# Four lengths in a kernel's own ordering model set to other values: top-k attention and a rational feed-forward layer on one core

## The chip, the core and the metric

The kernel runs on one core of a Trainium2 chip. The metric is device time in microseconds (us), the median of several executions. One execution was also recorded by the profiler; its rows are what the text reads.

## The reference

The inputs are q, k, v of shape (8 batches, 8 heads, 576 rows, 64), the weights of a layer (512 to 2048 to 512) in float64, and a few coefficients. Cut to what matters:

```python
scores = scale * np.matmul(q, k.transpose(0, 1, 3, 2))          # 576 x 576 per head
kth = np.partition(scores, -32, axis=-1)[..., -32:-31]
scores = np.where(scores >= kth, scores, -1e9)                   # keep the 32 largest of a row
attn = np.exp(scores - scores.max(-1, keepdims=True))
attn = attn / (attn.sum(-1, keepdims=True) + 1e-09)
x = (attn @ v).transpose(0, 2, 1, 3).reshape(4608, 512)
h = x @ w_in                                                     # 4608 x 2048
P = a[0] + a[1]*h + a[2]*h**2 + a[3]*h**3
Q = 1.0 + abs(b[0])*abs(h) + abs(b[1])*h**2
out = (P / (Q + 1e-6)) @ w_out
```

## The kernel before, in words

**Attention.** A tile is 128 query rows of one head (in a name `s_3_0_2_0`: batch 3, row block 0, head pair 2, head 0 of it); two tiles make a unit, and the last 64 rows of both heads make one mixed tile (row block 4). There are 288 tiles. TensorE makes the scores (L575, L572), ScalarE copies them out (`sb`, L582), and VectorE halves the row of 576 to two rows of 288, larger and smaller (`hi`, `lo`, L590 and L586), and takes the eight largest four times, striking them out between (L600, L606); L615 gives the 32nd. ScalarE makes the exponentials (`e`, L640), VectorE masks and sums them (`pr`, L643). TensorE turns `pr` (`trp`, L718 and L720; ScalarE copies out, `p`, L730) and multiplies it by the values (`av`, L744). There is one scores buffer, two `pr` buffers (one for each unit) and two PSUM banks of the tag `mm`, which `trp`, `av` and `ph` share. So the exponentials of a unit wait until all turns of the unit two before it are done.

**Feed-forward.** 256 rows of the attention's output are a chunk (`m2_2`: batch 2, row blocks 2 and 3; `t0`, `t4`: chunks of mixed rows). A chunk is done in eight groups of 256 hidden columns. A group is 24 matmuls into `ph` (L885; three split products for each of 4 x 2 pieces), three or four reads of `ph` by ScalarE, some five elementwise steps on GpSimd, VectorE and ScalarE, and a product with w_out: twelve matmuls for a group of split weights (L1038), four for one in full precision (L1031). From chunk 14 on (`y.late`) the elementwise chain has another form (L268 `hh`, L956 `va`, L959, L963 `pa` on VectorE; on GpSimd L967 and L968 in place of L963), and each step may be taken by more than one engine.

**Weights.** w_in and w_out are converted from float64 words at the start, in blocks of 128 x 512, by ScalarE (L387, L405), VectorE (L392, L399) and GpSimd (L409, L425).

**The order.** No engine's order is written out. `build` makes some twenty thousand steps; `Plan.run` (L83) then walks through them in a time of its own: a step has a length for each engine that may do it, a key (lower goes first), steps that it waits for, and buffers that it takes and gives. An engine that is free in that time takes the ready step of the lowest key whose buffers are free. What the walk decides is emitted: the order on each engine's queue and, where more than one engine may do a step, which one does it. The chip then runs each queue in that order, with its own durations. The lengths stand at L237 to L259, and some of them at the step itself.

The lengths that the change touches are: `pe_r` (L243), for scores (L652), hidden products (`add_group`) and split output products; `dma` (L246), for all transfers on the SP queue; the VectorE steps of the weight conversion in `weight_block` (L379 to L381, which no block of this kernel takes, and L414, L415); and `n_av` (L805), the value products of a unit pair.

```python
    pe_r = lambda n: max(0.107, n / 2400 + 0.003)
    dma = lambda n, words: max(0.52 * n, words * 4 / 180e3)
            m = add("PE", len(cs) * n_av, multiply(cs), [m] if m else pair.ev + [pair.vload], key + KEY['AV'],
```

## Time and profile before

| | |
|---|---|
| median of 3 runs | 1662.68 us (1662.24 to 1662.74) |
| the profiled execution | 1662.6 us, its span 1660.8 us |
| busy in the span: VectorE (DVE) | 1514.2 us, 91% |
| TensorE matmul (PE) | 1455.1 us, 88% |
| TensorE weight load (PEld) | 1138.5 us, 69% |
| ScalarE (ACT) | 1287.4 us, 78% |
| GpSimd (POOL) | 1286.2 us, 77% |
| mean granted TensorE clock | 0.954 |

Busy times are over the whole span, and stages differ: weights are converted in the first 300 us, then attention and feed-forward run side by side, and after the last attention tile (1554.5 us) only feed-forward is left. The span begins at the first recorded instruction; 1.8 us of the execution's time lie outside it.

### The profile page before, as it was taken

What the parts mean: (1) busy time and instruction counts of PE and PEld (TensorE: products, weight loads), DVE (VectorE), ACT (ScalarE), POOL (GpSimd) and SP (SyncE); (2) the same over time, 40 slices, a digit from 0 to 9 for tenths busy, and PEclk for the clock granted to TensorE, in tenths of its full rate; (3) what the DMA queues carried; (4) which work ended last, traced back from release to release, by engine and by line L of the source; (5) the groups of instructions that cost most, each with busy time, mean ns of one, the idle gap of its engine ahead of it and who ended that gap; (6) DMA issues with size and microseconds to landing.
All of it is one profiled execution on the core that took longest, in us unless ns stands there. A gap on an engine that the chain in (4) does not pass through costs nothing.

```text
span 1660.8 us, 31905 instructions
## 1 busy us (share of the span) xinstructions
PE 1455.1 (88%) x9513; PEld 1138.5 (69%) x9513; DVE 1514.2 (91%) x5044; ACT 1287.4 (78%) x2579; POOL 1286.2 (77%) x1649
## 2 busy tenths in 40 slices
PE   2436878899999899999999999998999999898996
PEld 1324656676777678777777777777777778676784
DVE  6989998999999999798899999999999999899753
ACT  4555857887888798787888888888788888777653
POOL 5675877787878698878877897988878988878642
PEclk9657888999999999999999999999999999999998
DMA  6454545334443454325443445344533554231122
GB/s 198 145 165 138 150 128 162 103 92 127 130 118 93 117 145 146 98 72 137 121 122 86 115 139 155 90 112 123 149 94 94 137 144 112 84 92 53 45 61 69
DMA packets 133238, 193.57 MB, mean 117 GB/s; under 512 B 21440, under 2 KB 71616, under 8 KB 133056
## 3 DMA queue, kind: packets, MB, share of 16 engines
q1 hardware_dynamic: 132992, 191.43, 40.6%
q8 instruction: 78, 1.28, 0.3%
q14 instruction: 104, 0.85, 0.2%
q0 software_dynamic: 64, 0.00, 0.0%
HBM read 125.83 MB, written 13.11 MB: 84 GB/s over the span
## 4 chain that ended last, share of the span: by engine, by line
PE 50%; DVE 27%; ACT 9%; POOL 6%; issue 4%; DMA 2%; SPq 1%; ACTq 0%; POOLq 0%; DVEq 0%
PE ph_m L885 14%; DVE m L600 9%; PE po_m L1038 8%; DVE hi L606 7%; PE av L744 7%; PE po_m L1031 6%; PE s L575 6%; PE trp L718 4%; DVE pr L643 4%; DVE lo L586 2%; PE ph_t L885 2%; DVE hi L590 2%; ACT p L730 2%; DVE w_w L399 1%; ACT e L640 1%
## 5 line engine op out<-in xcount | busy, mean ns | idle before, releaser
L600 DVE MAX8 m<-hi 128x8 f32<-128x288 f32 x1152 | 498.9, 451 | 2.4
L606 DVE MATCH_REPLACE8 hi<-m,hi 128x288 f32<-128x288 f32 x864 | 382.6, 445 | 0.1
L885 PE MATMUL ph_m<-xh_m,win_h 128*128 128x256 f32 x1024 | 309.9, 303 | 18.3 <-ACT p L730 12.9
L718 PE MATMUL trp<-ident,pr 128*128 128x128 f32 x1312 | 226.2, 285 | 80.9 <-DVE pr L643 50.2
L885 PE MATMUL ph_m<-xl_m,win_h 128*128 128x256 f32 x1024 | 288.2, 281 | 0.0
L885 PE MATMUL ph_m<-xh_m,win_l 128*128 128x256 f32 x1024 | 288.1, 281 | 0.0
L718 PEld LDWEIGHTS trp<-ident,pr 128*128 128x128 f32 x1312 | 162.9, 145 | 149.6 <-ACT p L730 45.1
L730 ACT COPY p<-trp 128x512 f32<-128x512 f32 (+1 forms) x448 | 227.2, 514 | 47.0 <-PE trp L718 35.7
L643 DVE SCALAR_TENSOR_TENSOR pr<-sb,m,e 128x576 f32<-128x576 f32 x288 | 231.0, 802 | 31.7 <-ACT e L640 29.4
L582 ACT COPY sb<-s 128x576 f32<-128x576 f32 x288 | 185.5, 644 | 95.5 <-PE s L575 81.1
L640 ACT ACTIVATE e<-sb,st 128x576 f32<-128x576 f32 x288 | 216.9, 753 | 40.1 <-DVE pr L643 36.5
L885 PEld LDWEIGHTS ph_m<-xh_m,win_h 128*128 128x128 f32 x1024 | 194.8, 190 | 41.9 <-ACT p L730 24.6
L885 PEld LDWEIGHTS ph_m<-xl_m,win_h 128*128 128x128 f32 x1024 | 195.2, 191 | 4.6 <-issue 3.3
L885 PEld LDWEIGHTS ph_m<-xh_m,win_l 128*128 128x128 f32 x1024 | 194.6, 190 | 0.0
L744 PE MATMUL av<-p,vm 128*64 128x256 f32 (+1 forms) x1920 | 189.1, 346 | 3.5 <-ACT p L730 2.3
L1031 PE MATMUL po_m<-wout,pa_m 128*128 128x512 f32 x384 | 187.8, 595 | 0.0
L907 POOL TENSOR_TENSOR pa_m<-pa_m,hh_m 128x512 f32<-128x512 f32 x104 | 133.9, 1288 | 50.3 <-ACT pa_m L904 49.2
L744 PEld LDWEIGHTS av<-p,vm 128*64 128x64 f32 x1920 | 112.5, 143 | 78.6 <-issue 16.5
L934 POOL TENSOR_TENSOR pa_m<-pa_m,va_m 128x512 f32<-128x512 f32 x104 | 134.1, 1289 | 29.6 <-ACT va_m L931 28.4
L575 PE MATMUL s<-ka,q 128*128 128x288 f32 x512 | 103.7, 327 | 50.0 <-DMA q<-qx 13.5
L590 DVE TENSOR_TENSOR hi<-s,sb 128x288 f32<-128x288 f32 x288 | 129.0, 448 | 17.6 <-ACT sb L582 16.8
L1038 PE MATMUL po_m<-wout,g_m 128*128 128x512 f32 x320 | 138.1, 431 | 1.6 <-ACT ob_m L1056 0.7
(143 smaller groups left out, 3678.2 us busy)
## 6 DMA issues: line engine op xcount, KB each, us to landing
wl_m<-wout_l SPq DMA_DIRECT2D x160, 256.0 KB, 2.7
vm<-in_v_dram SPq DMA_DIRECT2D x96, 320.0 KB, 3.0
q<-qx SPq DMA_DIRECT2D x128, 128.0 KB, 2.5
q<-qx SPq DMA_DIRECT2D x256, 64.0 KB, 2.1
km<-in_qk_dram SPq DMA_DIRECT2D x32, 352.0 KB, 3.3
kl<-in_qk_dram SPq DMA_DIRECT2D x32, 288.0 KB, 3.4
qx<-in_qk_dram SPq DMA_DIRECT2D x64, 128.0 KB, 2.8
w_w<-in_moe_w_in_dram SPq DMA_DIRECT2D x32, 256.0 KB, 3.9
```

The lines of the kernel that those rows point to most:

```text
L575: nc.tensor.matmul(s[:, hf, 0:HF], u.pair.q.q[:, i, t.h, o : o + P], kv.k[t.h][:, cols], start=(i == 0), stop=(i == 1),)
L582: nc.scalar.copy(t.sb, t.s[:, :, 0:HF])
L600: nc.vector.max(t.m[:, o : o + 8], getattr(t, src))
L606: nc.vector.match_replace(x, t.m[:, o : o + 8], x, NEG)
L640: nc.scalar.activation(t.e, t.sb, AF.Exp, scale=SCALE, bias=t.st)
L643: nc.vector.scalar_tensor_tensor(out=t.pr, in0=t.sb, scalar=t.kth, in1=t.e, op0=ALU.is_ge, op1=ALU.mult, accum_out=u.ss[:, t.h : t.h + 1],)
L718: nc.tensor.transpose(u.ps[i][:, c * P : (c + 1) * P], u.pr[:, x], ident)
L730: nc.scalar.copy(pair.pT[i][:, at].rearrange("p c n -> p (c n)"), u.ps[i][:, 0 : n * P])
L744: nc.tensor.matmul(pair.av[d, 0 : u.nq * len(pair.units)], lhs, x[:, 0, d] if u.mixed else x[:, 0] if lone else x, start=(c == 0), stop=(c ...
L885: nc.tensor.matmul(y.ph[:, f * NT : (f + 1) * NT], w[:, c, fs], z[:, c, :], start=(c == 0 and i == 0), stop=(c == HP - 1 and i == 2),)
L1031: nc.tensor.matmul(o.po[i], y.pa[:, at], wout[ff], start=(ff == 0), stop=(ff == NF - 1),)
L1038: nc.tensor.matmul(o.po[i], z, w, start=(ff == 0 and n == 0), stop=(ff == NF - 1 and n == 2),)
```

## The change

Lengths in the planner are set to other values; no instruction is added or removed, and no data is laid out otherwise.

```diff
-    pe_r = lambda n: max(0.107, n / 2400 + 0.003)
+    pe_r = lambda n: max(0.109, n / 2230 + 0.003)
-    dma = lambda n, words: max(0.52 * n, words * 4 / 180e3)
+    dma = lambda n, words: max(0.52 * n, words * 4 / 260e3)
...
-                    s1 = add("DVE", dve(128), upper, [ld], key + 1)
-                    s2 = add("DVE", dve(256), lower, [s1], key + 1)
-                    last.append(add("DVE", dve(256), ends, [s2], key + 2, give=hold if plain else []))
+                    s1 = add("DVE", 0.38, upper, [ld], key + 1)
+                    s2 = add("DVE", 0.5, lower, [s1], key + 1)
+                    last.append(add("DVE", 0.5, ends, [s2], key + 2, give=hold if plain else []))
...
-                s2 = add("DVE", dve(128), high, [s1], key + 1)
-                s3 = add("DVE", dve(256), low, [s2], key + 1)
+                s2 = add("DVE", 0.38, high, [s1], key + 1)
+                s3 = add("DVE", 0.5, low, [s2], key + 1)
...
-        n_av = 1.3 * pe_t if u.mixed else 2.5 * pe_t if lone else 4.42 * pe_t
+        n_av = 1.4 * pe_t if u.mixed else 2.7 * pe_t if lone else 4.6 * pe_t
```

What it does is move instructions, from the first rows on. Four counts change between engines: VectorE gets six more of the additions and products L956, four more L268 `hh` and two more L963, GpSimd six fewer L956; ScalarE passes 32 of the small scalings L272 on to GpSimd's L274. Three places:

**TensorE, the first feed-forward groups beside the mixed tiles of batch 0.** The rows just ahead of the last turn of the mixed tile `0_4_3`, up to that turn. Before:

```order
L885 MATMUL ph_m0_0_2_1640<-xh_m0_0_1352,win_l_79 128x256
L718 MATMUL trp0_0_4_3_1697<-ident_65,pr_0_4_3_1520 128x128 x4
L885 MATMUL ph_m0_0_2_1640<-xh_m0_0_1352,win_h_78 128x256
L885 MATMUL ph_m0_0_2_1640<-xl_m0_0_1353,win_h_78 128x256
L885 MATMUL ph_m0_0_2_1640<-xh_m0_0_1352,win_l_79 128x256
L575 MATMUL s_0_3_0_1_1712<-kb_0_0_132,q_0_0_2_1224 128x288 x4
L718 MATMUL trp2_0_4_3_1724<-ident_65,pr_0_4_3_1520 128x128
L720 MATMUL trp2_0_4_3_1724<-ident_65,rw_0_4_3_1634 128x128
```

Now:

```order
L885 MATMUL ph_m0_0_3_1839<-xh_m0_0_1351,win_l_79 128x256
L718 MATMUL trp0_0_4_3_1887<-ident_65,pr_0_4_3_1677 128x128 x4
L885 MATMUL ph_m0_0_3_1839<-xh_m0_0_1351,win_h_78 128x256
L885 MATMUL ph_m0_0_3_1839<-xl_m0_0_1352,win_h_78 128x256
L885 MATMUL ph_m0_0_3_1839<-xh_m0_0_1351,win_l_79 128x256
L885 MATMUL ph_m0_0_3_1839<-xh_m0_0_1351,win_h_78 128x256
L885 MATMUL ph_m0_0_3_1839<-xl_m0_0_1352,win_h_78 128x256
L885 MATMUL ph_m0_0_3_1839<-xh_m0_0_1351,win_l_79 128x256
L718 MATMUL trp2_0_4_3_1906<-ident_65,pr_0_4_3_1677 128x128
L720 MATMUL trp2_0_4_3_1906<-ident_65,rw_0_4_3_1848 128x128
```

The turn stood behind group 2 of the first chunk and stands behind group 3. Between the scores `s_0_3_0_0` and this turn there were 24 matmuls of `ph` and 10 rows of `av`; there are 48, with 12 of L1038 and 20 rows of `av`.

**TensorE, chunk m2_2, around the scores of the tile `3_1_2_0`.** Before:

```order
L1038 MATMUL po_m2_2_1_8751<-wl_m2_2_3_0_8884,g_m2_2_3_8886 128x512
L575 MATMUL s_3_1_2_0_8963<-ka_3_2_7495,q_3_2_0_8534 128x288 x4
L885 MATMUL ph_m2_2_7_8988<-xh_m2_2_8114,win_h_78 128x256
L885 MATMUL ph_m2_2_7_8988<-xl_m2_2_8115,win_h_78 128x256
L885 MATMUL ph_m2_2_7_8988<-xh_m2_2_8114,win_l_79 128x256
```

Now:

```order
L885 MATMUL ph_m2_2_6_8912<-xl_m2_2_8134,win_h_78 128x256
L885 MATMUL ph_m2_2_6_8912<-xh_m2_2_8133,win_l_79 128x256
L575 MATMUL s_3_1_2_0_8919<-ka_3_2_7533,q_3_2_0_8485 128x288 x4
L885 MATMUL ph_m2_2_6_8912<-xh_m2_2_8133,win_h_78 128x256
L885 MATMUL ph_m2_2_6_8912<-xl_m2_2_8134,win_h_78 128x256
```

At this tile the chunk stood at its last group, 7, and stands at group 6. Between the scores `s_3_0_2_0` and the last turn of unit `3_0_1` there were 57 matmuls of `ph` and 5 of L1031; there are 72 and 8 (L1038: 36 in both).

**VectorE, chunk m6_2, the rows that end with the masking of the tile `7_0_2_0`.** Before:

```order
L615 MAX m_7_1_2_19815<-m_7_1_2_19815 128x8
L963 SCALAR_TENSOR_TENSOR pa_m6_2_5_19851<-pa_m6_2_5_19851,co_70,va_m6_2_5_19848 128x512
L268 TENSOR_SCALAR hh_m6_2_6_19909<-va_m6_2_6_19900,co_70 128x512
L959 TENSOR_TENSOR pa_m6_2_6_19907<-pa_m6_2_6_19907,h_m6_2_6_19886 128x512
L963 SCALAR_TENSOR_TENSOR pa_m6_2_6_19907<-pa_m6_2_6_19907,co_70,h_m6_2_6_19886 128x512
L963 SCALAR_TENSOR_TENSOR pa_m6_2_6_19907<-pa_m6_2_6_19907,co_70,va_m6_2_6_19900 128x512
L959 TENSOR_TENSOR pa_m6_2_7_19944<-pa_m6_2_7_19944,h_m6_2_7_19932 128x512
L963 SCALAR_TENSOR_TENSOR pa_m6_2_7_19944<-pa_m6_2_7_19944,co_70,h_m6_2_7_19932 128x512
L963 SCALAR_TENSOR_TENSOR pa_m6_2_7_19944<-pa_m6_2_7_19944,co_70,va_m6_2_7_19941 128x512
L643 SCALAR_TENSOR_TENSOR pr_7_0_2_20019,ss_7_0_2_20020<-sb_7_0_2_0_19648,m_7_0_2_19703,e_7_0_2_0_20021 128x576
```

Now:

```order
L963 SCALAR_TENSOR_TENSOR pa_m6_2_5_19850<-pa_m6_2_5_19850,co_70,h_m6_2_5_19838 128x512
L963 SCALAR_TENSOR_TENSOR pa_m6_2_5_19850<-pa_m6_2_5_19850,co_70,va_m6_2_5_19843 128x512
L268 TENSOR_SCALAR hh_m6_2_6_19902<-va_m6_2_6_19892,co_70 128x512
L956 TENSOR_TENSOR va_m6_2_6_19892<-hh_m6_2_6_19902,va_m6_2_6_19892 128x512
L959 TENSOR_TENSOR pa_m6_2_6_19900<-pa_m6_2_6_19900,h_m6_2_6_19883 128x512
L963 SCALAR_TENSOR_TENSOR pa_m6_2_6_19900<-pa_m6_2_6_19900,co_70,h_m6_2_6_19883 128x512
L963 SCALAR_TENSOR_TENSOR pa_m6_2_6_19900<-pa_m6_2_6_19900,co_70,va_m6_2_6_19892 128x512
L268 TENSOR_SCALAR hh_m6_2_7_19939<-va_m6_2_7_19934,co_70 128x512
L956 TENSOR_TENSOR va_m6_2_7_19934<-hh_m6_2_7_19939,va_m6_2_7_19934 128x512
L963 SCALAR_TENSOR_TENSOR pa_m6_2_7_19937<-pa_m6_2_7_19937,co_70,h_m6_2_7_19930 128x512
L963 SCALAR_TENSOR_TENSOR pa_m6_2_7_19937<-pa_m6_2_7_19937,co_70,va_m6_2_7_19934 128x512
L643 SCALAR_TENSOR_TENSOR pr_7_0_2_20014,ss_7_0_2_20015<-sb_7_0_2_0_19498,m_7_0_2_19561,e_7_0_2_0_20016 128x576
```

All six L956 of the groups 2 to 7 come to VectorE here. Between the folding of the tile `7_0_2_0` and this masking VectorE does 13 more steps of the chain (six L956, five L963, three L268 more, one L959 fewer). On TensorE there were 96 matmuls of `ph`, 6 of L1031 and 30 of L1038 between the scores `s_7_0_2_0` and the last turn of unit `7_0_1`; there are 168, 11 and 36. Over the whole program the chunks start beside the same tiles as before, within six of them.

Two more counts: between the scores `s_0_2_3_0` and the last turn of unit `0_2_2` TensorE had 6 matmuls of `ph`, 4 of L1031, 10 rows of `av`, 12 of scores and other turns; now only two turns stand there. And behind the last turn of all (unit `7_3_3`) there were 294 matmuls of `ph` and 120 of L1038, and there are 288 and 114.

## Rows read from the trace of the kernel before

**Rows 1.** The page: the span, and busy time, share of the span and number of instructions of each engine.

```profile
span 1660.8 us, 31905 instructions
PE 1455.1 (88%) x9513; PEld 1138.5 (69%) x9513; DVE 1514.2 (91%) x5044; ACT 1287.4 (78%) x2579; POOL 1286.2 (77%) x1649
```

**Rows 2.** The page: the chain that ended last, shares of the span by engine.

```profile
PE 50%; DVE 27%; ACT 9%; POOL 6%; issue 4%; DMA 2%; SPq 1%; ACTq 0%; POOLq 0%; DVEq 0%
```

**Rows 3.** The view by stretches: start and end, length, busy time of each engine (and instructions), granted TensorE clock, DMA share, GB/s. The first three run from the first folding of scores to the end of the weight stage, from there to the last masking, and from there to the end; the others are two stretches inside the second of them, of chunk m2_2 and of chunk m6_2.

```profile
15.50:300.00 284.50, 173.63 (x983) 125.79 (x983) 263.80 (x831) 177.27 (x387) 195.41 (x280) 0.78 0.50 150
300.00:1554.50 1254.50, 1190.17 (x8019) 941.83 (x8019) 1200.36 (x4148) 1052.29 (x2094) 1041.67 (x1324) 0.99 0.40 113
1554.50:1660.80 106.30, 89.99 (x508) 69.93 (x507) 48.80 (x63) 54.23 (x95) 40.67 (x29) 0.95 0.21 61
690.00:710.00 20.00, 16.96 (x95) 11.60 (x94) 8.08 (x27) 13.31 (x26) 17.68 (x20) 0.97 0.34 90
1380.00:1450.00 70.00, 63.97 (x432) 51.54 (x432) 62.46 (x189) 53.46 (x106) 58.98 (x64) 1.00 0.35 100
```

**Rows 4.** Waits of VectorE, longest first in total: who waited for whom, us in total, times, longest.

```profile
DVE pr L643 <- ACT e L640: 29.4, 10, 10.7
```

**Rows 5.** The timeline of VectorE in chunk m2_2: start, us, instruction, and idle time before it with its releaser.

```profile
691.36 0.09 DVE L606 MATCH_VALUE_LOAD hi<-m,hi 128x8 f32 x1
691.79 0.46 DVE L600 MAX8 m<-hi 128x8 f32<-128x288 f32 x1
692.15 0.45 DVE L600 MAX8 m<-lo 128x8 f32<-128x288 f32 x1
692.51 0.17 DVE L615 MAX8 m<-m 128x8 f32<-128x16 f32 x1
692.59 0.46 DVE L600 MAX8 m<-hi 128x8 f32<-128x288 f32 x1
...
695.19 0.18 DVE L615 MAX8 m<-m 128x8 f32<-128x16 f32 x1
706.08 0.81 DVE L643 SCALAR_TENSOR_TENSOR pr<-sb,m,e 128x576 f32<-128x576 f32 x1 [10.71 <-ACT e L640]
```

**Rows 6.** The timeline of TensorE in the same place. The first two are the first and the last of eleven matmuls of `ph` in a row, the next two of six of L1038; the last but one is of the ten rows of `av`, each two passes.

```profile
689.79 0.28 PE L885 MATMUL ph_m<-xl_m,win_h 128*128 128x256 f32 x1
...
690.97 0.28 PE L885 MATMUL ph_m<-xh_m,win_l 128*128 128x256 f32 x1
...
693.02 0.39 PE L1038 MATMUL po_m<-wout,g_m 128*128 128x512 f32 x1
...
694.18 0.40 PE L1038 MATMUL po_m<-wl_m,g_m 128*128 128x512 f32 x1
694.42 3.60 PE L1031 MATMUL po_m<-wout,pa_m 128*128 128x512 f32 x8
697.95 2.38 PE L744 MATMUL av<-p,vm 128*64 128x256 f32 x20
...
704.34 0.27 PE L720 MATMUL trp<-ident,rw 128*128 128x128 f32 x1
```

**Rows 7.** Groups of VectorE's instructions by line and shape: count, busy time and mean ns of one, idle time before them and its releaser.

```profile
L963 DVE SCALAR_TENSOR_TENSOR pa_m<-pa_m,co,h_m 128x512 f32<-128x512 f32 x18 | 22.2, 1234 | 15.5 <-POOL pa_m L959 15.4
L963 DVE SCALAR_TENSOR_TENSOR pa_m<-pa_m,co,va_m 128x512 f32<-128x512 f32 x18 | 17.1, 947 | 5.4 <-ACT va_m L931 3.9
L956 DVE TENSOR_TENSOR va_m<-hh_m,va_m 128x512 f32<-128x512 f32 x14 | 9.7, 691 | 0.8
L268 DVE TENSOR_SCALAR hh_m<-va_m,co 128x512 f32<-128x512 f32 x15 | 9.0, 601 | 22.1 <-ACT va_m L950 22.1
```

**Rows 8.** One line of the code, L956: number, shortest, median and longest ns, and the first and the last start in us.

```profile
L956 DVE TENSOR_TENSOR va_m<-hh_m,va_m x14: 682/692/693, 1555.4 to 1638.3; 128x512 f32<-128x512 f32 x14
L956 POOL TENSOR_TENSOR va_m<-hh_m,va_m x10: 1268/1300/1649, 1385.2 to 1550.4; 128x512 f32<-128x512 f32 x10
```

**Rows 9.** The timeline of TensorE in the weight stage: the `av` of a mixed tile (its ten rows, two passes each), and the first matmul of the groups 1, 2, 3 and 4 of chunk m0_0.

```profile
159.92 0.80 PE L744 MATMUL av<-p,vm 128*64 128x64 f32 x20 [0.81 <-ACT p L730]
...
163.50 0.28 PE L885 MATMUL ph_m<-xh_m,win_h 128*128 128x256 f32 x1
...
172.61 0.42 PE L885 MATMUL ph_m<-xh_m,win_h 128*128 128x256 f32 x1
...
179.96 0.39 PE L885 MATMUL ph_m<-xh_m,win_h 128*128 128x256 f32 x1 [0.46 <-ACT p L730]
...
199.90 0.39 PE L885 MATMUL ph_m<-xh_m,win_h 128*128 128x256 f32 x1 [0.72 <-ACT p L730]
```

**Rows 10.** The timeline of VectorE later in the weight stage, at the maskings of the tiles `0_2_3_0` and `0_2_3_1`.

```profile
253.29 0.81 DVE L643 SCALAR_TENSOR_TENSOR pr<-sb,m,e 128x576 f32<-128x576 f32 x1 [2.82 <-ACT e L640]
...
255.11 0.81 DVE L643 SCALAR_TENSOR_TENSOR pr<-sb,m,e 128x576 f32<-128x576 f32 x1 [1.00 <-ACT e L640]
```

**Rows 11.** The end: VectorE's last masking (its timeline), and TensorE's last matmuls (its timeline).

```profile
1554.51 0.82 DVE L643 SCALAR_TENSOR_TENSOR pr<-sb,m,e 128x576 f32<-128x576 f32 x1
...
1644.21 3.60 PE L1031 MATMUL po_m<-wout,pa_m 128*128 128x512 f32 x8
```

**Rows 12.** Groups of VectorE's instructions in the weight conversion: count, busy time, mean ns of one, idle time before.

```profile
L399 DVE SCALAR_TENSOR_TENSOR w_w<-w_w 128x256 int32<-128x256 int32 x64 | 38.0, 613 | 0.0
L392 DVE TENSOR_SCALAR w_w<-w_w 128x256 int32<-128x256 int32 x64 | 28.8, 468 | 15.4 <-ACT w_w L387 14.7 <-issue 0.7
```

## The prediction

> **What bounds the kernel now.** I read the busy times first, then the chain that ended last, then the stretches, and last the timelines where VectorE stands still. VectorE is busy for 1514.2 us of 1660.8, TensorE's matmuls for 1455.1 [rows 1], so two engines look like the bound, and the chain puts half of its time on TensorE [rows 2]. The stretches part them. From 15.5 to 300 us VectorE is busy for 263.8 of 284.5 us and TensorE for only 173.6; from 300 us to the last masking VectorE for 1200.4 of 1254.5; after it VectorE has 48.8 of 106.3 and TensorE 90.0 [rows 3]. So VectorE sets when attention ends, at 1554.5 us, and what feed-forward work is then left on TensorE sets the rest, up to the last matmuls at 1644.2 us [rows 11]. That TensorE's busy time overstates it is seen in its own rows: a matmul of `ph` is counted as 0.28 us, but eleven of them start 0.118 us apart (1.18 us for ten steps); six of L1038 start 0.232 us apart, and eight of L1031 fill 3.53 us until `av` starts, 0.44 each [rows 6].
>
> The Trainium skill (Perfetto Trace Analysis, Identifying the Most-Contended Engine) says that matmul busy time is a poor measure of TensorE and its weight load time a good one, and to take the engine of the highest occupancy otherwise. By that rule VectorE with 91% is the bound against 69% of weight loads, as the stretches have it; were the 88% believed, the first term below would fall out, and the sum would be 12.4 - 8.7 = 3.7, so 1666.3 us.
>
> What VectorE still loses in the long middle stretch lies in a few places. The largest is chunk m2_2: it has nothing to do from the end of a small maximum at 695.4 until 706.1 us, 10.7 us [rows 5], and waits of this kind, a masking for ScalarE's exponentials, come to 29.4 us in ten times [rows 4]. The exponentials wait in turn for a `pr` buffer, which is free when TensorE has done the last turn of the unit two before; that turn ends at 704.6 us, behind 3.53 us of L1031 and the ten rows of `av` [rows 6]. So the quantity to follow in the two orders is this: between a tile's scores and the turn that frees its `pr` buffer, how much does TensorE have to do, and how much has VectorE to do meanwhile? What the first has more than the second is a stall.
>
> **The change part by part.** Lengths of the planner cost nothing on the chip; all comes through the order. How near they are to the rows: three split products are now 0.354 us in the planner (0.330 before), and the rows say 3 x 0.118; the conversion steps are 0.38 and 0.5 us, where the rows have 468 and 613 ns [rows 12], so nearer but still short; ten rows of `av` become 2.51 us (2.41 before), and the row says 2.38, so that one is no nearer [rows 6]. For the transfers no row separates the queue's own time, and I take no gain or loss from it; what is moved on SP's queue is the order of weight blocks, which lies in the same stage as the fourth and fifth terms.
>
> 1. *More work on VectorE.* Six L956 come from GpSimd, at 691 ns: 4.15 us. Four L268 at 601 ns: 2.40 us. Two L963, at the mean of 1234 and 947 ns: 2.18 us [rows 7]. All stand ahead of the last masking, since the fourteen L956 that VectorE has now start at 1555.4 us and later [rows 8] and stay. Together 8.7 us. If VectorE were idle there anyway, part would be free: in the stretch of m6_2 it is idle for 70.0 - 62.5 = 7.5 us [rows 3]. So 1.2 to 8.7. I take 8.7, because that idle time comes from TensorE's run ahead of the turn, which grows by as much (third term).
>
> 2. *Chunk m2_2.* Between the scores and the turn there are 15 matmuls of `ph` more (15 x 0.118 = 1.77 us) and three L1031 (3 x 0.44 = 1.32 us), 3.1 us in all, while VectorE's rows in between are of the same kinds and numbers. The stall is there already, so nothing covers it: 10.7 becomes 13.8 us. TensorE itself is idle for 20.0 - 17.0 = 3.0 us of this stretch [rows 3]; if the new matmuls fell into that, 0.1 would be left. So 0.1 to 3.1, and 3.1 taken.
>
> 3. *Chunk m6_2.* TensorE has 72 matmuls of `ph`, five L1031 and six L1038 more ahead of the turn: 8.5 + 2.2 + 1.4 = 12.1 us. VectorE has 13 more steps in between: six L956, three L268, and five L963 less one step (priced as an L963): 4.15 + 1.80 + 4.36 = 10.3 us, which the first term has paid for. What is left is 1.8 us. TensorE is idle for 6.0 us of 70 there [rows 3], so it could be nothing; with no cover by VectorE it would be 12.1. I take 1.8.
>
> 4. *A new stall in the weight stage.* Ahead of the turn of `0_4_3` TensorE now has 48 matmuls of `ph` (5.7 us), 12 L1038 (2.8), two `av` of mixed tiles (1.6, [rows 9]), and 22 turns and scores at about 0.118 (2.6, an estimate): 12.7 us. VectorE has in between four foldings and six maxima at 0.36 us from start to start, four strikings-out at 0.43, one small maximum of 0.08 [rows 5], two maskings of 0.82, and five short steps, which I put at 0.17 each like the small maximum: 3.6 + 1.7 + 0.1 + 1.6 + 0.9 = 7.9 us. The difference is 4.7 us (with the unrounded parts). Nothing, if TensorE is already ahead; or more, since in this stage groups 1 to 3 began 9.1 and 7.4 us apart [rows 9], not the 2.8 us of 24 matmuls: two groups at that pace are 16.5 us, 8.6 more than VectorE's 7.9. So 0 to 8.6, and 4.7 taken.
>
> 5. *A stall that goes.* At 253 us two maskings wait, 2.82 and 1.00 us [rows 10]. They wait for the turn of `0_2_2`, ahead of which almost all of TensorE's work is gone. Minus 3.8 us; nothing, if that feed-forward work holds up another turn.
>
> 6. *The end.* Behind the last turn TensorE has six `ph` and six L1038 fewer: 0.7 + 1.4 = 2.1 us, minus; nothing, if the end is held by the chain from group to group.
>
> The sum is 8.7 + 3.1 + 1.8 + 4.7 - 3.8 - 2.1 = **12.4 us**. It is made against the profiled execution of 1662.6 us, which is 0.1 us from the median of the runs, so **1675.0 us**. About 0.2%, some 3.3 us, is what a measurement of this kernel can tell from no change; the forecast is well outside it.
>
> **The rivals.** *Cover (faster).* VectorE's new steps fill the 7.5 us in which it is idle beside m6_2, TensorE's longer runs fill its own idle 3.0 and 6.0 us, and the weight stage has no new stall. Then it is 1.2 + 0.1 + 0 + 0 - 3.8 - 2.1 = -4.6 us: 1658.0 us. The place is 1380 to 1450 us, and it decides from the point where more than some 5 us of the 8.7 are free. For it: L956 takes 0.69 us on VectorE and 1.30 on GpSimd [rows 8], so the chain that TensorE waits for gets shorter. Against it: 72 more `ph` in the same run.
>
> *Slow groups (slower still).* The weight stage goes by the pace of its groups, 8.6 for 4.7, and the stall at 253 us is not saved, only moved: 8.7 + 3.1 + 1.8 + 8.6 - 2.1 = 20.1 us, 1682.7 us. For it: the distances of [rows 9], and a granted clock of 0.78 in that stage [rows 3]. Against it: the weight blocks that made the pace are converted earlier now.
>
> *Little (no change).* VectorE's work is covered as in the first rival, but the stalls on TensorE are not: 1.2 + 3.1 + 0 + 4.7 - 3.8 - 2.1 = 3.1 us, 1665.7 us. This is also what comes if the planner's new lengths do not do what they say: three of four are not what the rows show, and the skeleton of chunks beside tiles is the same.
>
> **How the numbers follow.** The forecast has 0.45: its first term is a count of instructions at measured durations on the engine that bounds, which is the firmest thing here. Slow groups have 0.20, cover 0.20, little 0.15. Slower by over 0.2% is the forecast and the slow groups, 0.65; within 0.2% the little, 0.15; faster by over 0.2% the cover, 0.20. The range reaches from cover, 1658, with a microsecond below it, to all terms at their upper ends, 8.7 + 3.1 + 1.8 + 8.6 + 0 + 0 = 22.2 us, 1685: 1657 to 1685 us. The forecast's own range is 1669 to 1681. Left out are the two outer cases of terms three and four, and rearrangements elsewhere that I have not priced.
>
> **What would show it.** Right: VectorE busy for some 8 us more; the last masking at about 1569 us; the wait in m2_2 near 14 us; a wait of some 5 us at a masking around 190 us and none at 253; the end some 104 us after the last masking. Wrong: VectorE's idle time down in 1380 to 1450 us by as much as its work rises (cover), or a last masking earlier than 1554.5 us. The sum is also wrong if VectorE loses or gains in places not named: the wait for L959 and the foldings' waits for ScalarE are spread over the whole run and are taken as unchanged.

## The result, and the profile after

The changed kernel takes 1676.7 us (median of five, 1672.7 to 1677.4) against 1662.7 for the kernel before on the same chip: ratio 1.0071, 95% interval 1.0055 to 1.0088 (the ratio is estimated from all runs, so it is not the quotient of the two medians, which lie 13.9 us apart). The forecast was 1675.0 us, and slower. The profiled execution took 1674.4 us. Its page, first the span and the busy times, then the chain that ended last [rows 1, 2]:

```profile
span 1672.3 us, 31952 instructions
PE 1461.3 (87%) x9513; PEld 1133.8 (68%) x9513; DVE 1513.5 (91%) x5056; ACT 1284.3 (77%) x2541; POOL 1285.1 (77%) x1673
DVE 39%; PE 25%; ACT 11%; POOL 10%; issue 6%; DMA 5%; SPq 4%; POOLq 0%; ACTq 0%; DVEq 0%
```

The stretches, columns as in [rows 3], with the last masking now at 1564.69 us:

```profile
15.50:300.00 284.50, 176.60 (x1005) 130.29 (x1004) 261.48 (x824) 178.86 (x388) 206.11 (x292) 0.79 0.51 153
300.00:1564.69 1264.69, 1195.25 (x8011) 934.57 (x8011) 1202.90 (x4166) 1048.49 (x2053) 1028.33 (x1335) 0.99 0.40 111
1564.69:1672.30 107.61, 88.69 (x500) 68.11 (x498) 47.86 (x63) 53.96 (x95) 43.42 (x32) 0.95 0.21 60
```

The middle is 10.2 us longer, the end 1.3. The table goes finer: starts of maskings in us, found by setting each kernel's order beside its trace (the span's start is zero). Each kernel has one such execution; how far two of them lie apart is shown with the fifth run below.

| masking of tile | before | after | difference | gained or lost since the row above |
|---|---|---|---|---|
| `3_4_3_0` | 646.1 | 647.6 | +1.4 | +1.4 |
| `3_0_2_0` (behind chunk m2_2) | 706.1 | 714.0 | +7.9 | +6.5 |
| `7_0_0_1` | 1388.2 | 1382.3 | -5.9 | -13.8 |
| `7_0_2_0` (behind chunk m6_2) | 1445.0 | 1458.8 | +13.8 | +19.7 |
| `7_3_3_1`, the last | 1554.5 | 1564.7 | +10.2 | -3.6 |
| end of the span | 1660.8 | 1672.3 | +11.5 | +1.3 |

In m2_2 VectorE's timeline (start, us, instruction, idle time before it) answers to [rows 5]:

```profile
697.17 0.18 DVE L615 MAX8 m<-m 128x8 f32<-128x16 f32 x1
713.99 0.81 DVE L643 SCALAR_TENSOR_TENSOR pr<-sb,m,e 128x576 f32<-128x576 f32 x1 [16.64 <-ACT e L640]
```

and TensorE's to [rows 6]; it begins with the last hidden product of m2_2 and ends with the turn that frees `pr`:

```profile
698.53 0.28 PE L885 MATMUL ph_m<-xh_m,win_l 128*128 128x256 f32 x1
...
700.06 0.50 PE L1038 MATMUL po_m<-wl_m,g_m 128*128 128x512 f32 x1 [0.79 <-DMA wl_m<-wout_l]
...
701.10 3.60 PE L1031 MATMUL po_m<-wout,pa_m 128*128 128x512 f32 x8
704.62 2.38 PE L744 MATMUL av<-p,vm 128*64 128x256 f32 x20
708.34 0.66 PE L718 MATMUL trp<-ident,pr 128*128 128x128 f32 x4 [1.34 <-ACT x_m L761]
...
712.16 0.27 PE L720 MATMUL trp<-ident,rw 128*128 128x128 f32 x1
```

The wait grew from 10.71 to 16.64 us. The new wait in the weight stage is there, in two parts, and the maskings that waited at 253 us [rows 10] wait no longer (last row, the first of them):

```profile
192.66 0.46 DVE L771 TENSOR_TENSOR xm<-av,p 64x64 f32<-64x64 f32 x2 [3.81 <-PE av L744]
200.12 0.81 DVE L643 SCALAR_TENSOR_TENSOR pr<-sb,m,e 128x576 f32<-128x576 f32 x1 [7.00 <-ACT e L640]
...
257.28 0.80 DVE L643 SCALAR_TENSOR_TENSOR pr<-sb,m,e 128x576 f32<-128x576 f32 x1
```

The end answers to [rows 11]. TensorE's last matmuls in its timeline (the last masking is at 1564.69):

```profile
1655.53 3.60 PE L1031 MATMUL po_m<-wout,pa_m 128*128 128x512 f32 x8
```

VectorE's groups (count, busy, mean ns, idle before), which answer to [rows 7, 12], have the counts foretold, but not the means:

```profile
L399 DVE SCALAR_TENSOR_TENSOR w_w<-w_w 128x256 int32<-128x256 int32 x64 | 38.3, 623 | 0.0
L392 DVE TENSOR_SCALAR w_w<-w_w 128x256 int32<-128x256 int32 x64 | 30.1, 485 | 16.2 <-ACT w_w L387 15.8
L963 DVE SCALAR_TENSOR_TENSOR pa_m<-pa_m,co,h_m 128x512 f32<-128x512 f32 x19 | 20.3, 1068 | 19.2 <-POOL pa_m L959 19.2
L956 DVE TENSOR_TENSOR va_m<-hh_m,va_m 128x512 f32<-128x512 f32 x20 | 15.7, 786 | 1.4
```

### The profile page after: what moved, and what is told of

Same layout as the page of the kernel before. It is cut to its first block, busy times and chain, and to the rows that moved or that the text cites. A ratio compares the mean times of both kernels' runs of the same rounds, so it can differ in the third digit from the quotient of the medians.

```text
span 1672.3 us, 31952 instructions
## 1 busy us (share of the span) xinstructions
PE 1461.3 (87%) x9513; PEld 1133.8 (68%) x9513; DVE 1513.5 (91%) x5056; ACT 1284.3 (77%) x2541; POOL 1285.1 (77%) x1673
## 4 chain that ended last, share of the span: by engine, by line
DVE 39%; PE 25%; ACT 11%; POOL 10%; issue 6%; DMA 5%; SPq 4%; POOLq 0%; ACTq 0%; DVEq 0%
DVE m L600 12%; DVE hi L606 10%; DVE pr L643 6%; PE ph_m L885 6%; PE av L744 4%; PE s L575 4%; DVE hi L590 3%; PE trp L718 3%; PE po_m L1038 3%; DVE lo L586 3%; PE po_m L1031 2%; SPq L527 2%; DVE w_w L399 1%; ACT p L730 1%; POOL pa_m L959 1%
## 5 line engine op out<-in xcount | busy, mean ns | idle before, releaser
L606 DVE MATCH_REPLACE8 hi<-m,hi 128x288 f32<-128x288 f32 x864 | 380.3, 442 | 0.1
L885 PE MATMUL ph_m<-xh_m,win_h 128*128 128x256 f32 x1024 | 310.1, 303 | 16.5 <-ACT p L730 8.2
L718 PEld LDWEIGHTS trp<-ident,pr 128*128 128x128 f32 x1312 | 159.3, 145 | 152.5 <-ACT p L730 36.9
L744 PE MATMUL av<-p,vm 128*64 128x256 f32 (+1 forms) x1920 | 191.5, 349 | 2.6 <-ACT h_m L910 2.6
L1031 PE MATMUL po_m<-wout,pa_m 128*128 128x512 f32 x384 | 185.8, 594 | 0.6 <-POOL pa_m L968 0.5
L744 PEld LDWEIGHTS av<-p,vm 128*64 128x64 f32 x1920 | 113.8, 144 | 81.8 <-issue 20.8
L1038 PE MATMUL po_m<-wout,g_m 128*128 128x512 f32 x320 | 139.8, 437 | 2.0 <-ACT ob_t L1056 1.3
```

The costliest lines, as they stand in the source:

```text
L606: nc.vector.match_replace(x, t.m[:, o : o + 8], x, NEG)
L718: nc.tensor.transpose(u.ps[i][:, c * P : (c + 1) * P], u.pr[:, x], ident)
L744: nc.tensor.matmul(pair.av[d, 0 : u.nq * len(pair.units)], lhs, x[:, 0, d] if u.mixed else x[:, 0] if lone else x, start=(c == 0), stop=(c ...
L885: nc.tensor.matmul(y.ph[:, f * NT : (f + 1) * NT], w[:, c, fs], z[:, c, :], start=(c == 0 and i == 0), stop=(c == HP - 1 and i == 2),)
L1031: nc.tensor.matmul(o.po[i], y.pa[:, at], wout[ff], start=(ff == 0), stop=(ff == NF - 1),)
L1038: nc.tensor.matmul(o.po[i], z, w, start=(ff == 0 and n == 0), stop=(ff == NF - 1 and n == 2),)
```

## The experiments

Three theories stood against each other. *Waits*: the time follows the pieces in which TensorE has more to do between scores and turn than VectorE. *Count*: it follows VectorE's number of steps. *Redraw*: any change of a length draws a new order, and all such orders cost about as much as the changed kernel, near 1677 us. Times are medians. Behind each stands its ratio to the kernel before, run beside it on the same chip, with the 95% interval in brackets; on the three chips used, before took 1663.0 us (first four runs), 1664.7 (next four) and 1664.0 (last four).

**One part of the change at a time, on the kernel before**, in this order, one in each of four kernels:

```diff
-    pe_r = lambda n: max(0.107, n / 2400 + 0.003)
+    pe_r = lambda n: max(0.109, n / 2230 + 0.003)
...
-    dma = lambda n, words: max(0.52 * n, words * 4 / 180e3)
+    dma = lambda n, words: max(0.52 * n, words * 4 / 260e3)
...
-        n_av = 1.3 * pe_t if u.mixed else 2.5 * pe_t if lone else 4.42 * pe_t
+        n_av = 1.4 * pe_t if u.mixed else 2.7 * pe_t if lone else 4.6 * pe_t
...
-                s2 = add("DVE", dve(128), high, [s1], key + 1)
-                s3 = add("DVE", dve(256), low, [s2], key + 1)
+                s2 = add("DVE", 0.38, high, [s1], key + 1)
+                s3 = add("DVE", 0.5, low, [s2], key + 1)
```

> Only the length of the split products is changed (2230 for 2400, 0.109 for 0.107). In its order, against before, TensorE's work between a tile's scores and the turn it waits for, less VectorE's work in the same piece, grows by 0.9 us at unit 3_0_1, 3.2 at 3_1_1, 2.7 at 7_0_1 and 1.4 at 7_1_1, and falls by 2.9 at 3_3_1; summed over all units +1.4. VectorE has five more steps ahead of the last masking (three of them L956), +2.5 us; TensorE has 5.4 us less behind the last turn. Theory waits (the time is the waits that such pieces make): +1.4 - 5.4 = 1659 us. Theory count (VectorE's extra steps): 1665. Theory any redraw (every other set of lengths costs about as much): near 1677.

> Only the transfers are made shorter in the planner (260e3 for 180e3). Against before: pieces 3_0_1 -0.2, 3_1_1 +2.5, 3_3_1 some -3, 7_0_1 +1.4, 7_1_1 -0.4 us, summed -0.6; VectorE has nine more steps ahead of the last masking, +7.0 us; TensorE 1.4 us less behind the last turn. Theory waits: 1661 us. Theory count: 1669.5. Theory any redraw: near 1677. This run parts the first two best.

> Only the value products are made longer (4.6, 2.7 and 1.4 for 4.42, 2.5 and 1.3). Against before: pieces 3_0_1 -0.6, 3_1_1 +2.4, 4_4_2 some +5, 4_4_0 and 4_4_1 some +3 each, 7_0_1 +1.2, 7_1_1 +0.7 us, summed +10.7; VectorE's work ahead of the last masking -0.2 us; TensorE 1.9 us less behind the last turn. Theory waits: 1671 us. Theory count: 1662.5. Theory any redraw: near 1677.

> Only the two conversion steps are made longer (0.38 and 0.5). Its order differs from before only inside the weight stage; from there on the pieces and VectorE's count are those of before to the step. Theories waits and count: 1662.7, within 2 us. Theory any redraw: near 1677.

Measured: split products 1651.1 us (0.993 [0.9916, 0.9944]), transfers 1642.8 (0.9878 [0.986, 0.9897]), values 1663.9 (1.000 [0.999, 1.001]), conversion 1658.4 (0.9961 [0.9944, 0.9977]). No theory holds. The first two are faster than either theory of sizes had them, by 8 and 18 us, the fourth by 4; the third stands with count. None comes near 1677, as redraw had it. Nor do the parts add: -11.9 - 20.3 + 0.9 - 4.7 makes 36 us faster, and together they are 14 slower. All four are early already at masking `3_4_3_0`, the first row of the table above: 636.2, 626.8, 636.5 and 639.0 us, for 646.1 before and 647.6 in the changed kernel. A weaker form of redraw, that the time of each new order is luck, is left open by these runs.

**The products of m6_2 back on GpSimd, in the changed kernel.**

```diff
-            engine().tensor_tensor(out=y.va, in0=y.hh, in1=y.va, op=ALU.mult)
+            eng = nc.gpsimd if nm.startswith("m6_2_") else engine()
+            eng.tensor_tensor(out=y.va, in0=y.hh, in1=y.va, op=ALU.mult)
```

> The changed kernel with its own order, but the products L956 of chunk m6_2 are issued to GpSimd, as six of them were before. VectorE has six steps of 691 ns fewer in the stretch from the masking of tile 7_0_0_1 to that of 7_0_2_0 (76.5 us in the changed kernel, 56.9 before). Theory count (VectorE's steps set the time there): that stretch 4.1 us shorter, about 1672.5 us. Theory TensorE's run (the masking waits for the turn behind feed-forward anyway): the time stays at 1676.7 and VectorE's idle time in the stretch rises by 4 us. If the longer steps on GpSimd (1.30 us) hold up the chain, up to 4 us slower, 1680.

Measured: 1681.6 us (1.0105 [1.0088, 1.0122]). The changed kernel has 1.0071 [1.0055, 1.0088], so this is slower by some 0.3%, with the two intervals just meeting, and nearest to the third case expected. The stretch from masking `7_0_0_1` to `7_0_2_0`, by the view by stretches, in the changed kernel:

```profile
1382.30:1458.80 76.50, 66.88 (x433) 53.10 (x432) 59.97 (x163) 51.71 (x100) 54.26 (x54) 1.00 0.29 83
```

and with the products on GpSimd:

```profile
1387.30:1468.00 80.70, 68.62 (x433) 54.68 (x432) 56.17 (x157) 51.57 (x100) 59.27 (x60) 0.98 0.28 78
```

VectorE is busy for 3.8 us less and the stretch is 4.2 longer: the steps on VectorE were not what it cost, and count falls as a price. What grew is TensorE's wait ahead of the chunk's group 5, for ScalarE to read an earlier `ph` (L904); first the changed kernel, then with the products on GpSimd:

```profile
1426.54 0.38 PE L885 MATMUL ph_m<-xh_m,win_h 128*128 128x256 f32 x1 [2.10 <-ACT pa_m L904]
1432.41 0.39 PE L885 MATMUL ph_m<-xh_m,win_h 128*128 128x256 f32 x1 [3.31 <-ACT pa_m L904]
```

That the chain to which the products belong costs the time fits this, but is not shown for all of it: 1.9 of the 4.2 us lie behind the chunk's last hidden product, in an execution whose granted clock in the stretch was 0.98 for 1.00.

The run also shows how far two executions of one program lie apart. Up to the products of m6_2 it is the changed kernel, instruction for instruction; yet masking `7_0_0_1` comes 5.0 us later (1387.3 for 1382.3). Between 749 and 855 us it lost 5.2 us, where its granted clock was lower, a mean between the two levels of 1.2 and 2.4 GHz. First the changed kernel, then this one:

```profile
760.00:820.00 60.00, 54.60 (x362) 42.44 (x358) 52.82 (x184) 49.28 (x97) 53.49 (x66) 1.00 0.48 135
760.00:820.00 60.00, 53.71 (x324) 41.20 (x325) 49.19 (x171) 45.47 (x89) 49.60 (x61) 0.91 0.46 128
```

So a difference of some 5 us between the traces of two kernels, late in the run, need not come from their orders. Distances within one trace, and medians, are firmer.

**A second buffer for `x`.**

```diff
-        "k": 4, "kr": 1, "km": 1, "q": 2, "qr": 1, "v": 3, "sb": 3, "lo": 1, "hi": 2,
+        "k": 4, "kr": 1, "km": 1, "q": 2, "qr": 1, "v": 2, "sb": 3, "lo": 1, "hi": 2,
...
-        "x": 1, "xm": 1, "xs": 1, "t": 9, "ob": 1, "wl": 2,
+        "x": 2, "xm": 1, "xs": 1, "t": 9, "ob": 1, "wl": 2,
...
-                        u.m = buf("m", [P, 2, 64], F32, f"m_{u.nm}")
+                        u.m = buf("m", [P, 2, 48], F32, f"m_{u.nm}")
...
```

(Left out: two lines of a path that is not taken, which use columns of `m` that are still there.)

> The changed kernel with a second buffer for a chunk's input x, with room made for it (two in place of three buffers of values; 48 for 64 columns of the maxima, which are all that this path uses). The first value product of chunk m3_0 (and of m7_0) takes x, which the chunk of mixed rows t0 (t4) holds until chunk m2_2 (m6_2) has done its last hidden product. In its order no piece is left in which TensorE has more to do than VectorE between scores and turn; VectorE has 17 us less ahead of the last masking; TensorE has 43 us more behind the last turn (115 for 72). Theory buffer (one x is why the turns stand behind feed-forward): the waits of 16.6 us at tile 3_0_2_0, 5.1 at 3_2_2_0 and 4.1 at 7_0_2_0 go, the stretch 7_0_0_1 to 7_0_2_0 falls from 76.5 to about 45 us, the last masking comes 40 to 50 us earlier, and some 40 of that are given back at the end: 1655 to 1675 us. Theory feed-forward load (TensorE is just full there): the waits stay above 10 us, elsewhere or there, and the time at 1676 or above.

> The kernel before with the second buffer for x, made in the same way. Pieces with a wait go from 22.1 to 2.5 us in all; VectorE has 11 us less ahead of the last masking; TensorE has 22 us more behind the last turn (96 for 74). Theory buffer: the waits of 10.7 and 9.0 us go, the last masking 30 us earlier, the end about 1650 us. Theory feed-forward load: near 1663 or above.

Measured: the changed kernel with it 1670.9 us (1.004 [1.0026, 1.0054]), the kernel before with it 1634.5 (0.9811 [0.9791, 0.9831]), 15 us faster than expected. VectorE's waits for the exponentials, in the changed kernel

```profile
DVE pr L643 <- ACT e L640: 35.2, 7, 16.6
```

([rows 4] before; us in total, times, longest) are, in the changed kernel with two buffers,

```profile
DVE pr L643 <- ACT e L640: 2.0, 3, 1.1
```

and there the stretch that took 76.5 us takes 37.9, with VectorE busy for 37.83 of it:

```profile
1362.50:1400.40 37.90, 37.30 (x219) 28.45 (x217) 37.83 (x136) 30.39 (x59) 30.80 (x42) 1.00 0.38 108
```

The waits are the buffer's: theory buffer holds. The first value product of m3_0 (L744) takes `x`; `t0` has it until its split, which takes `xs`, which m2_2 gives back with its last hidden product. The last masking of the changed kernel comes 53.7 us earlier (1511.0), and 50.2 of these are given back behind it (157.8 us for 107.6), where feed-forward is left over.

But the change's loss is not the buffer's. With two buffers the change costs 36.4 us (1670.9 for 1634.5), with one 13.9. Feed-forward is late with either: with two buffers the last hidden product of m6_2 ends at 1462.6 us with the change and at 1434.0 without it.

**A constant moved by 0.4%.**

```diff
-    pe_r = lambda n: max(0.107, n / 2400 + 0.003)
+    pe_r = lambda n: max(0.107, n / 2410 + 0.003)
```

> The kernel before with one constant of the planner moved by 0.4% (2410 for 2400 in the length of split products), which says nothing about the chip. Theory redraw (as the parts alone have it: the order of the weight stage is drawn anew by any change of a length, and its time with it): the first three quarters of the weight stage, to the masking of tile 0_2_3_0, moves by 5 us or more against before's 253.3, either way, and the total by as much. Theory lengths (only what the lengths say matters): within 2 us of before up to there. Later its order has a longer piece at 3_1_1 (+2.5 us), 7_0_1 (+4.4) and 7_1_1 (+1.1), and 5.8 us less on TensorE behind the last turn: about the same in all, 1663.

Measured: 1665.4 us (1.0004 [0.9993, 1.0015]), and masking `0_2_3_0` at 252.9 us for 253.3. So not every redraw moves the weight stage. But the middle moves: 6.1 us late at `3_0_2_0`, 6.8 early at `7_0_0_1`, 4.1 late at `7_0_2_0`, the shape of the changed kernel from a change that means nothing (of the last two, some 5 us can come from the execution alone, as shown above).

**The new stall taken out of the changed kernel.**

```diff
-                add_chunk(u.closes, moe_at + KEY['MS'] * u.closes.n, KEY['PACE'])
+                add_chunk(u.closes, moe_at + KEY['MS'] * u.closes.n + (90 if u.closes.n == 0 else 0), KEY['PACE'])
```

> The changed kernel with the key of the first chunk m0_0 raised by 90, so that its groups 2 and 3 stand behind the mixed tiles of batch 0 again; the last 2324 of TensorE's 2720 planned steps and the last 2995 of VectorE's 3869 are in the order of the changed kernel. Piece 0_4_3 is 5.8 us shorter, nothing else changes. Theory stall (this piece is what the changed kernel loses in the weight stage): the waits of 3.8 and 7.0 us at 189 to 200 us go, the lead at the masking of 0_2_3_0 falls from +4.0 us to -2 or below, and everything behind keeps its distances (16.6 at 3_0_2_0, 19.6 more up to 7_0_2_0): 1667 to 1671 us. Theory conversion (the stage goes by the conversion steps, 485 and 623 ns each): under 2 us gained, 1675 or above.

Measured: 1676.6 us (1.0074 [1.0062, 1.0087]). The two waits are gone but for this one:

```profile
188.03 0.81 DVE L643 SCALAR_TENSOR_TENSOR pr<-sb,m,e 128x576 f32<-128x576 f32 x1 [1.86 <-ACT e L640]
```

Masking `0_2_3_0` comes 4.4 us earlier than in the changed kernel, not the 6 or more that theory stall expected, and the total is as theory conversion had it (1675 or above). "Everything behind keeps its distances" was wrong: this kernel is 4.1 us ahead of the changed one at `3_0_2_0`, 0.9 at `3_3_2_1` (806.9 us), and not at all at the end. In this execution, too, the granted clock was lower than the changed kernel's where the lead was lost:

```profile
760.00:820.00 60.00, 54.16 (x336) 43.10 (x337) 49.56 (x170) 45.03 (x88) 49.94 (x61) 0.91 0.42 116
```

So the two traces do not show what the order alone would have kept. The times show no gain that is clear of noise (1.0074 for 1.0071).

**The changed kernel less one part**: the conversion steps at their old lengths, then (another kernel) the split products.

```diff
-                s2 = add("DVE", 0.38, high, [s1], key + 1)
-                s3 = add("DVE", 0.5, low, [s2], key + 1)
+                s2 = add("DVE", dve(128), high, [s1], key + 1)
+                s3 = add("DVE", dve(256), low, [s2], key + 1)
...
-    pe_r = lambda n: max(0.109, n / 2230 + 0.003)
+    pe_r = lambda n: max(0.107, n / 2400 + 0.003)
```

> The changed kernel without the new lengths of the conversion steps. Its order has no long piece at 0_4_3, but one at 1_4_3 (+7.0 us); 3_0_1 and 3_1_1 are longer still (+4.4 and +7.4 us against before), and 7_0_1 and 7_1_1 (+5.2, +3.8); VectorE has 11.2 us more ahead of the last masking and TensorE 6.8 us less behind the last turn. Theory stall: some 10 us ahead of the changed kernel up to 0_2_3_0, some 5 of them lost again at 1_4_3, and a wait of 19 to 22 us at 3_0_2_0: 1668 to 1680 us. Theory conversion: the stage is as long as that of the changed kernel, and the total near 1685.

> The changed kernel without the new length of split products. VectorE has 6.1 us more than before ahead of the last masking (changed: 8.4); waits in pieces sum to 30.4 us (before 22.1, changed 38.6); 3_0_1 and 3_1_1 +2.2 and +4.4, 7_0_1 and 7_1_1 +2.4 and +1.8 us against before. Theory waits and count: 3 to 8 us less than the changed kernel, 1669 to 1674. Theory redraw (the weight stage decides): as for the parts alone, up to 15 us less, 1662.

Measured: 1661.3 us (0.9978 [0.9967, 0.9989]) and 1675.1 (1.0061 [1.0037, 1.0085]). Without the conversion lengths the loss is gone, though alone they gain 4.7 us; the first expectation was some 7 us too high at its lower end. Against the changed kernel that order is 25.4 us early at masking `0_2_3_0` (231.9 for 257.3), 5.0 at `3_0_2_0`, 15.0 at `7_0_0_1` and 13.6 at the end of the span. The second is just outside the range that waits and count gave.

**What the runs point to**: the kernel before with the diff of the second buffer above, 11.354 for 71.354 as `MOE` and 40.0 for 53.562 as `PJ` in KEY (keys of feed-forward's groups and of their output products; lower goes first), and

```diff
-    dma = lambda n, words: max(0.52 * n, words * 4 / 180e3)
+    dma = lambda n, words: max(0.52 * n, words * 4 / 260e3)
```

> What the runs point to, put together: before with the second buffer for x, the shorter transfers alone, and feed-forward moved forward in the planner (MOE 11.354 for 71.354, PJ 40 for 53.562). No piece with a wait over half a microsecond is left in its order; VectorE has 14.4 us less than before ahead of the last masking, TensorE 19.3 us more behind the last turn. If the gains add (before with two x is 30 us faster, shorter transfers 20): 1605 to 1625 us. If they share the same waits, near 1634.

Measured: 1621.4 us (0.9739 [0.9725, 0.9754]), 2.6% faster than before. Buffer and transfers alone gave 30 and 20 us; this is 43. It is not shown how much of the 43 the moved keys give, which were not tried alone.

## Why the prediction was right, and where its steps were not

The time came out within 1.7 us, the sign by the case that was given most. Its steps did not fare as well, and that the sum fits is in part luck.

**First term, more work on VectorE (8.7 us).** The count is right: priced at the mean of each kind in the trace of before, VectorE has some 9 us more ahead of the last masking (net six L956, three L963 and three L268). "VectorE busy some 8 us more" is not there (1513.5 for 1514.2), since nearly every kind of step was a little shorter in that execution (below). And the price fails: the argument that VectorE's steps lengthen m6_2 is contradicted by the run that took six of them away there and became slower, and VectorE stood idle for 16.5 of the 76.5 us of that stretch.

**Second, chunk m2_2 (3.1 us).** The mechanism is right, the size too small: between the scores `s_3_0_2_0` and the turn TensorE took 26.4 us and takes 32.5. The term priced an L1031 at half. It counted three of them in the order and took 0.44 us for each from [rows 6]; but each L1031 of the order is two rows of the trace, so that the eight rows there are the four of one group, and one takes 0.88 us. The 15 products and three L1031 are then 1.8 + 2.6 = 4.4 of the 6.1. TensorE's waits inside the run grew by 1.4, from 1.4 to 2.8 (among them 0.79 for a weight block and 1.34 for the copy of `av`, in the rows above); 0.3 remain.

**Third, chunk m6_2 (1.8 us, with the first 10.5).** The stretch grew by 19.7, and the whole of it is TensorE's run, as the term's mechanism has it: from the scores `s_7_0_2_0` to the turn it was 33.4 us and is 53.0. The size is wrong in two places. At 0.88 us the five L1031 are 4.4 us, so the added matmuls are 14.3 of these 19.6 and not 12.1; and TensorE's waits, which the term thought might take some of this up, grew by 4.6 (from 4.0 to 8.6). The same stretch of before, to be set beside the first row shown with the fifth run:

```profile
1388.20:1445.00 56.80, 51.62 (x324) 41.33 (x324) 50.28 (x148) 42.21 (x86) 51.48 (x56) 1.00 0.33 93
```

VectorE is busy for 9.7 us more, near the 10.3, but idle for 10.0 more (16.5 for 6.5), where the term had 1.8. Why the run sets the time, and not VectorE, is seen when the end of the chunk's hidden products is set beside the masking that waits for it, and beside the span's end:

| kernel | masking `7_0_0_1` | m6_2's last hidden product ends | masking `7_0_2_0`, after that | end, after that |
|---|---|---|---|---|
| transfers alone | 1358.9 | 1412.3 | 15.8 | 228.7 |
| split products alone | 1370.4 | 1419.7 | 15.8 | 226.8 |
| before | 1388.2 | 1429.6 | 15.5 | 231.2 |
| after | 1382.3 | 1443.3 | 15.5 | 229.0 |
| after, stall out | 1381.4 | 1442.9 | 15.5 | 231.0 |
| products on GpSimd | 1387.3 | 1450.6 | 17.4 | 232.6 |
| before, two `x` | 1353.8 | 1434.0 | -46.4 | 200.0 |
| after, two `x` | 1362.4 | 1462.6 | -62.3 | 206.1 |

In all eleven orders with one `x` the masking comes 15.4 to 19.6 us after that product and the end 227 to 233 us after it, wherever attention stood at `7_0_0_1`. With two the masking no longer waits for the product, and the end still follows it, by 200 to 206 us. So the prediction's "VectorE sets when attention ends" is what fails: with one `x`, feed-forward sets it there, through the buffer. In the changed kernel m6_2 begins 22.8 us later (1397.0 for 1374.2) and ends 13.7 later, and masking `7_0_2_0` is 13.8 later.

The rows of the changed kernel there, TensorE's last hidden product of m6_2, `av` and the turns:

```profile
1443.03 0.28 PE L885 MATMUL ph_m<-xh_m,win_l 128*128 128x256 f32 x1
...
1448.60 2.38 PE L744 MATMUL av<-p,vm 128*64 128x256 f32 x20
...
1454.12 0.66 PE L718 MATMUL trp<-ident,pr 128*128 128x128 f32 x4 [2.25 <-ACT x_m L761]
...
1457.25 0.27 PE L720 MATMUL trp<-ident,rw 128*128 128x128 f32 x1
```

Here is GpSimd's first step of the split of `t4`, which that product releases, before and after (the split's last step, GpSimd's second L848, ends at 1436.5 and 1449.6 us):

```profile
1429.66 1.01 POOL L268 TENSOR_SCALAR xh_t<-x_t 128x512 fp32r<-128x512 f32 x1 [1.04 <-PE ph_m L885]
1443.41 0.67 POOL L268 TENSOR_SCALAR xh_t<-x_t 128x512 fp32r<-128x512 f32 x1 [1.46 <-PE ph_m L885]
```

VectorE's masking starts 1.6 us after the start of the last turn:

```profile
1458.81 0.81 DVE L643 SCALAR_TENSOR_TENSOR pr<-sb,m,e 128x576 f32<-128x576 f32 x1 [4.08 <-ACT e L640]
```

**What the sum left out.** The 13.8 us that attention gained between `3_0_2_0` and `7_0_0_1` were a loan: TensorE did attention first and feed-forward later. It was paid back in m6_2. (In the two other traces with the changed kernel's order there, the gain was 10.1 and 10.6 us, so the 13.8 is not exact.) Taken as one piece from `3_0_2_0` to the last masking, the change is +2.3 us (10.2 - 7.9); the terms had 10.5 there. That the sum is right owes much to errors that cancel: 0.5 us too little in the weight stage, 3.4 in m2_2 (6.5 for 3.1) and 3.4 at the end (1.3 for -2.1), against 8.2 too much in between. With an L1031 at 0.88 us the same terms would have made 15.9 us and 1678.5.

**Fourth and fifth, the weight stage (4.7 - 3.8 = 0.9).** The net is right, +1.4 at 646 us. The new stall was larger than its piece, 10.8 us in two waits; taking it out was worth 4.4 us at masking `0_2_3_0`, near the 4.7, and nothing that could be measured at the end. The lead was down to 1.0 us when chunk m3_0's last hidden product ended (871.1 us for 872.1), in an execution with a lower clock there, so what took it is not shown. Nor is it shown that the stall is part of the 14 us.

**Sixth, the end (-2.1 us).** It is +1.3: twelve matmuls fewer did not shorten it.

**The rivals.** Little and cover fall with the time, and so do the slow groups: the stage kept its length. None of them had the buffer. What stays open is why just this combination lets feed-forward fall 22.8 us behind ahead of m6_2, when the transfers alone bring m6_2 15.1 us forward (1359.1 for 1374.2). The traces show where: after chunk m4_2 the two kernels are level (last hidden products at 1121.5 us for 1121.7), after m5_0 the changed one is 12.5 us late (1218.2 for 1205.7), after m6_0 31.5 (1391.5 for 1360.0), while attention goes from some 3 us late to 3 us early. The runs show that the parts do not add, and that conversion lengths in company cost 15 us; how these lengths, whose steps end by 220 us, come to a lag at m5_0 is not shown, and luck of the order is not shut out. The changed kernel less its new transfers, or less its new value products, was not tried.

## What to carry to other kernels

Where two streams of work share one buffer at their seam, follow the buffer, not the busiest engine: set the end of the last user beside the first step that waits for it in several orders, and a constant distance names what the step waits for. Then take the buffer away: here the waits went, and the change's loss did not. In these orders a lead won ahead of such a seam was a loan; add up terms from seam to seam, not stall by stall. And a planner's length that comes nearer to a trace's mean need not give a better order: parts that gain alone can lose together, so time them one by one and in company. Last, before reading a few us out of two traces, set two executions of one program side by side.

## What the runs showed of the hardware

A conversion step has no one length. L392 and L399 of the changed kernel (shortest, median and longest ns):

```profile
L392 DVE TENSOR_SCALAR w_w<-w_w x64: 271/296/1372, 11.2 to 219.5; 128x256 int32<-128x256 int32 x64
L399 DVE SCALAR_TENSOR_TENSOR w_w<-w_w x64: 403/420/1509, 12.5 to 220.0; 128x256 int32<-128x256 int32 x64
```

The longest L392 in VectorE's timeline

```profile
212.04 1.37 DVE L392 TENSOR_SCALAR w_w<-w_w 128x256 int32<-128x256 int32 x1
213.47 0.43 DVE L606 MATCH_REPLACE8 hi<-m,hi 128x288 f32<-128x288 f32 x1
```

ends 0.15 us after GpSimd's product in the same timeline:

```profile
211.80 1.46 POOL L934 TENSOR_TENSOR pa_m<-pa_m,va_m 128x512 f32<-128x512 f32 x1 [2.76 <-ACT va_m L931]
```

With no GpSimd work beside them, 17 of the 64 L392 took 291 ns on average. The selection steps show nothing of the kind (L606: 433 to 452 ns from the 5th to the 95th of a hundred). The Trainium skill (Trainium Architecture — The Big Picture, What this means for kernel authors) says that VectorE and GpSimd contend for a shared port pair, as an exclusive lock; these rows agree. So the mean of L392 depends on the order: 485 ns here, 374 with the transfers alone

```profile
L392 DVE TENSOR_SCALAR w_w<-w_w 128x256 int32<-128x256 int32 x64 | 23.1, 374 | 14.5 <-ACT w_w L387 13.9 <-DMA wl_m<-wout_l 0.3
```

which is 7 us of VectorE in the weight stage. A mean from a trace, as the change sets it, is the mean of one order.

Last, all selection steps share a small drift between profiled executions, whatever the kernel: MAX8 takes 450 ns on average in the trace of before, 447 in that of after, 449 to 451 on the chip of the four parts and 445 to 447 on that of the last four runs. On 1500 us of VectorE 0.7% is 10 us, as much as the effect looked for, so busy times of two executions are compared by counts.
